# Attention and two MLP layers on one core: the softmax's division moved from the weights to the output

## The chip, the cores and the metric

The kernel runs on one core of a Trainium2 chip. The metric is the device time of one execution in microseconds (us), lower is better. The core's engines are named as the profile names them: PE (matrix multiply; PEld are its weight loads), DVE (vector), ACT (scalar), POOL (GpSimd) and SP, whose queue issues the transfers.

## The reference

```python
q_rot, k_rot = (rotate(q), rotate(k))          # rotary embedding, 4 x 8 heads, 576 positions, 64 wide
scores = scale * np.matmul(q_rot, k_rot.transpose(0, 1, 3, 2))
scores = scores - np.max(scores, axis=-1, keepdims=True)
attn = np.exp(scores)
attn = attn / (np.sum(attn, axis=-1, keepdims=True) + 1e-09)
x = np.matmul(attn, v)                         # then 2304 tokens x 512
h = x @ w_in;  x = elu(h) @ w_out              # layer 1, d_ff 2048
h = x @ w_in2; out = (h - np.tanh(h)) @ w_out2 # layer 2, d_ff 2048
```

All inputs and the output are float32.

## The kernel before

**Attention.** The 32 heads are taken as 16 pairs. A pair has nine items (`items`): four blocks of 128 query rows for each of its two heads, and one item of 128 rows that holds the last 64 rows of both. The loop over `i` goes through all 144 items, and each turn writes out a few steps of several items, so that the engines' queues are staggered. In turn i these are, in this order: the row maximum of item i on DVE (`emit_max`), the copies out of PSUM that the last turn left over (`flush`), the score matmuls of item i+1 (`emit_s`, tile s), the exponential of item i on ACT with its row sum `den` (`emit_exp`, tile a), the normalization of item i-1 (`emit_norm`), parts of the rotary work of later pairs (`prep`), the transposes of item i-D on PE into PSUM tiles pt and pr (`emit_t`, D = 4), and the products with v for a finished group of rows (`emit_pv`, tile o). The order on each engine's queue is the order of this loop; `sched` says in which turn a pair's loads and prep steps stand.

`emit_norm` runs once for two items (one at the pair's end): DVE adds 1e-9 to the two row sums (L243) and takes their reciprocals (L244), and POOL multiplies the 128x576 weights of each head in place (L247). The copies out of PSUM (L261 on DVE, L263 on ACT) are dealt out in turn, six of a pair's fifteen to DVE. The attention output o leaves PSUM as two float32r parts: ACT casts it to `xh` (L274), and a turn later DVE subtracts to get `xl` (L266). These two are the layers' input. A prep is five steps for q and five for k of a pair: two multiplications with the rotary tables (L143, mostly POOL), their sum on DVE (L145), a float32r copy on ACT (L148) and the remainder on DVE (L153), and the result goes by transfers to the places from which PE reads it.

**Layers.** Each of 192 steps takes 384 tokens and 128 of d_ff: 12 matmuls over the parts `xh`, `xl` (`emit_f1`, L441), the activation on ACT, DVE and POOL, and four steps later the second product (`emit_f2`, L498 in layer 1, L500 in layer 2). `conv_w` turns the weights into two float32r parts (L77 to L97); eight of these conversions lie in attention, over two pairs each.

Of the kernel before, what the change touches and what calls it, by code (L numbers as in the profile page):

```python
# [24 lines left out]
def attention_elu_tanhshrink(ctx: ExitStack, tc: tile.TileContext, qk, v, w1i, w1o, w2i, w2o, tab, out):  # L25
# [76 lines left out]
    with ExitStack() as actx:  # L102
# [17 lines left out]
        def load_qk(p, x):  # L120
            if p == 1 and x == 0:
                t = p3.tile([128, 2, S], F32, tag="a", name="t0")
            else:
                t = (p1, p2)[x].tile([128, 2, S], F32, tag=f"t{x}", name=f"t{x}")
            nc.sync.dma_start(out=t, in_=qk[p, :, 2 * x:2 * x + 2, :])
            t_t[p, x] = t
# [6 lines left out]
        def prep(p, x, i):  # L133
            t = t_t[p, x]
            mul = SCALE if p > 0 and x == 0 else 1.0
            if i < 2:
                if p == 0 and x == 0:
                    nc.vector.scalar_tensor_tensor(
                        out=t[:, i, :], in0=t[:, i, :], scalar=SCALE, in1=tabs[:, i, :], op0=ALU.mult, op1=ALU.mult
                    )  # L140
                else:
                    eng = nc.vector if p < 2 and i == 1 else nc.gpsimd
                    eng.tensor_tensor(out=t[:, i, :], in0=t[:, i, :], in1=tabs[:, i, :], op=ALU.mult)  # L143
            elif i == 2:
                nc.vector.tensor_tensor(out=t[:, 0, :], in0=t[:, 0, :], in1=t[:, 1, :], op=ALU.add)  # L145
            elif i == 3:
                hl_t[p, x] = p1.tile([128, 2, S], F32R, tag=f"hl{x}", name=f"hl{x}")
                nc.scalar.mul(hl_t[p, x][:, 0, :], t[:, 0, :], mul)  # L148
# [86 lines left out]

        def emit_norm(i):
# [20 lines left out]
        def flush():  # L257
# [6 lines left out]
            late.clear()  # L264
            for x0, hp, o, n in late_l:
                nc.vector.tensor_tensor(  # L266
                    out=xl[:, hp, x0:x0 + n], in0=o[:, 0:n], in1=xh[:, hp, x0:x0 + n].bitcast(F32),
                    op=ALU.subtract,
                )
            late_l.clear()  # L270
            for p, grp, o, n in late_x:
                b, hp = divmod(p, 4)
                x0 = b * S + 256 * grp
                nc.scalar.copy(out=xh[:, hp, x0:x0 + n], in_=o[:, 0:n])  # L274
                late_l.append((x0, hp, o, n))
            late_x.clear()

        def emit_t(i):
# [3 lines left out]
            if (u % 2 == 0) and h in (0, None):  # L282
                if grp < 2:
                    aT_t[p, grp] = (p2.tile([128, 2, 4, 256], F32, tag="aT", name="aT"),
                                    p2.tile([128, 256], F32, tag="aTr", name="aTr"))
                else:
                    aT_t[p, grp] = (p1.tile([128, 2, 4, 64], F32, tag="aT2", name="aT2"),
                                    p1.tile([128, 64], F32, tag="aTr2", name="aTr2"))
            aT, aTr = aT_t[p, grp]
# [5 lines left out]
            if h is None:  # L295
                for hh in range(2):
                    evac(aT[:, hh, :, 0:64], pt[:, :, 64 * hh:64 * hh + 64])
                pr = ps_t.tile([128, 4, 128], F32, tag="pt", name="pr")
                for hh in range(2):
                    sl = slice(64 * hh, 64 * hh + 64)  # L300
                    nc.tensor.matmul(out=pr[sl, 0, 0:64], lhsT=a[sl, 0, 512:576], rhs=ident[sl, sl],
                                     start=True, stop=True)
                evac(aTr[:, 0:64], pr[:, 0, 0:64])
                return
            evac(aT[:, h, :, q0:q0 + 128], pt)
            if h == 1:
                pr = ps_t.tile([128, 4, 128], F32, tag="pt", name="pr")
                nc.tensor.transpose(pr[:, 0, :], a.rearrange("p h s -> p (h s)")[:, 512:640], ident)
                evac(aTr[:, q0:q0 + 128], pr[:, 0, :])

        o_t = {}

        def emit_pv(p, grp, c):
# [6 lines left out]
            for h in range(2):  # L320
# [3 lines left out]
                else:  # L324
                    w, m = vt[sl, 512:576], aTr[sl, 0:n]
                nc.tensor.matmul(out=o[sl, 0:n], lhsT=w, rhs=m, start=(c == 0), stop=(c == 4))  # L326
# [4 lines left out]
            if grp == 2:  # L331
                v_t.pop(p)
            late_x.append((p, grp, o, n))
# [6 lines left out]
        early = {1: ((None, 0, 0, 1, 2, 3), (None, 0, 0, 0, 1, 2)), 2: ((2, 4, 5, 7, 7, 8), (4, 7, 9, 11, 12, 13))}  # L340
        for p in range(1, NPAIR):
            i0 = NI * (p - 1)
            for x in range(2):
                when = [i0 + o for o in ((-8, -6, -4, -3, -2, -1), (-7, -2, 0, 2, 3, 4))[x]]
                if p in early:
# [6 lines left out]
        with tc.manual_schedule():  # L352
            for x in range(2):
                t = t_t[0, x] = (p1, p2)[x].tile([128, 2, S], F32, tag=f"t{x}", name=f"t{x}")
                for i in range(2):
# [76 lines left out]
    def emit_f1(i):  # L432
# [72 lines left out]
    def emit_acc():  # L505
        while y_done:
            l, g, t, ys = y_done.pop()
            for e, y in enumerate(ys):
# [11 lines left out]
                if l == 0:  # L520
                    xs = slice(NB * t, NB * t + NB)
                    nc.scalar.copy(out=xh[:, e, xs], in_=a)
                    nc.gpsimd.tensor_tensor(
                        out=xl[:, e, xs], in0=a, in1=xh[:, e, xs].bitcast(F32), op=ALU.subtract
                    )
                else:
# [6 lines left out]
    with tc.manual_schedule():  # L533
# [80 lines left out]
```

## Time and profile before

| | |
|---|---|
| median of 3 runs | 1145.89 us (1145.56 to 1146.97) |
| the profiled execution, its own time | 1145.03 us |
| its span, first to last instruction | 1143.2 us |
| attention, up to the unbroken run of layer 1's matmuls | 0 to 325.06 us |
| PE busy, share of the span | 1100.3 us, 96% |
| DVE | 844.6 us, 74% |
| ACT | 612.9 us, 54% |
| POOL | 655.9 us, 57% |

The page's shares are means over two stages that are unlike each other. PE's busy time has modelled ends, so that neighbouring matmuls overlap in it; a near-full PE there isn't a proof that it never waits. For a stage the windows, the chain of waits and the timeline are read.

### The profile page before, as it was taken

The page shows a single profiled execution, that of the slowest core. Times are in us where ns is not written, and L with a number is a line of the kernel's source. Part 1 is how long each engine was busy: PE and PEld are TensorE (multiplying, and loading weights), DVE is VectorE, ACT ScalarE, POOL GpSimd, SP SyncE. Part 2 cuts the span into 40 slices and gives each one's busy share as a digit, 9 for nine tenths or more (in the row PEclk, how much of TensorE's full clock was granted, in tenths as well). Part 3 has the DMA queues.
Part 4 walks back from the last instruction along what each step waited for, and adds up shares of the span by engine and source line. Part 5 has one row for each costly group of instructions (what it writes and reads, how often), then busy time and mean ns, then how long its engine had stood idle before and what let it go on. Part 6 is the DMA issues. An engine that isn't in the chain of part 4 may idle for free.

```text
span 1143.2 us, 18404 instructions
## 1 busy us (share of the span) xinstructions
PE 1100.3 (96%) x6656; PEld 982.2 (86%) x6656; DVE 844.6 (74%) x1477; ACT 612.9 (54%) x1383; POOL 655.9 (57%) x585
## 2 busy tenths in 40 slices
PE   2899999999999999999999999999999999999998
PEld 2677776777789999999999999988999888999997
DVE  6998889888744334545544566898899999999775
ACT  3677777767634433333333343657766565655553
POOL 3877787778433333333333555866666566666553
PEclk9999999999999999999999999999999999999999
DMA  7767776766211111111111111011111111110102
GB/s 235 192 191 193 200 178 189 205 189 176 71 38 38 37 56 38 37 53 41 38 37 57 37 38 53 22 38 56 38 38 37 38 47 47 38 38 1 56 31 81
DMA packets 29627, 91.96 MB, mean 80 GB/s; under 512 B 4192, under 2 KB 4192, under 8 KB 29536
## 3 DMA queue, kind: packets, MB, share of 16 engines
q1 hardware_dynamic: 29536, 90.78, 27.6%
q8 instruction: 53, 0.87, 0.3%
q14 instruction: 38, 0.31, 0.1%
HBM read 57.74 MB, written 4.72 MB: 55 GB/s over the span
## 4 chain that ended last, share of the span: by engine, by line
PE 72%; DVE 21%; POOL 2%; ACT 2%; issue 1%; DMA 1%; SPq 1%; DVEq 0%; ACTq 0%
PE h L441 28%; PE y L498 17%; PE y L500 11%; PE o L326 6%; PE s L208 5%; PE pt L294 4%; DVE nm L217 3%; DVE f L476 3%; DVE w L475 2%; DVE f L84 2%; DVE aT L261 2%; DVE f L80 1%; DVE acc L517 1%; DVE hl L153 1%; DVE mask L474 1%
## 5 line engine op out<-in xcount | busy, mean ns | idle before, releaser
L441 PE MATMUL h<-xh,w 128*128 128x384 f32 x1536 | 424.1, 337 | 0.0
L483 POOL TENSOR_TENSOR g<-f,g 128x384 fp32r<-128x384 f32 x192 | 215.6, 1124 | 240.3 <-ACT g L482 240.2
L441 PEld LDWEIGHTS h<-xh,w 128*128 128x128 f32 x1536 | 281.7, 188 | 4.4
L441 PE MATMUL h<-xl,w 128*128 128x384 f32 x768 | 258.2, 336 | 0.0
L500 PE MATMUL y<-w,g 128*128 128x512 f32 x864 | 219.2, 399 | 7.7 <-DVE acc L517 4.6
L498 PE MATMUL y<-g,w 128*128 128x384 f32 x1152 | 215.2, 336 | 0.0
L498 PEld LDWEIGHTS y<-g,w 128*128 128x128 f32 x1152 | 201.1, 188 | 0.0
L500 PEld LDWEIGHTS y<-w,g 128*128 128x128 f32 x864 | 161.8, 189 | 40.0 <-DVE acc L517 5.7
L247 POOL TENSOR_SCALAR a<-a,r 128x576 f32<-128x576 f32 x144 | 132.2, 931 | 67.6 <-DVE r L244 49.9
L482 ACT CAST g<-f 128x384 fp32r<-128x384 f32 x192 | 99.3, 517 | 133.3 <-PE y L498 94.6
L468 DVE TENSOR_SCALAR f<-f 128x384 f32<-128x384 f32 x96 | 39.2, 408 | 147.9 <-ACT f L450 147.9
L441 PEld LDWEIGHTS h<-xl,w 128*128 128x128 f32 x768 | 144.6, 188 | 4.2
L458 POOL TENSOR_TENSOR q<-q,u 128x384 f32<-128x384 f32 x96 | 110.5, 1151 | 55.7 <-ACT q L457 55.5
L97 POOL TENSOR_TENSOR w<-f,w 128x512 fp32r<-128x512 f32 x64 | 87.9, 1374 | 90.7 <-ACT w L96 90.3
L217 DVE TENSOR_REDUCE nm<-s 128x1 f32<-128x576 f32 x144 | 108.0, 750 | 33.9 <-PE s L208 33.0
L231 ACT ACTIVATE a<-s,nm 128x576 f32<-128x576 f32 x144 | 107.5, 747 | 40.4 <-DVE nm L217 31.9
L450 ACT ACTIVATE f<-h 128x384 f32<-128x384 f32 x96 | 47.3, 492 | 147.8 <-PE h L441 141.0
L517 DVE TENSOR_TENSOR acc<-y,acc 128x384 f32<-128x384 f32 (+1 forms) x126 | 72.8, 611 | 47.1 <-PE y L498 40.8
L476 DVE COPY_PREDICATED f<-mask,w 128x384 f32<-128x384 uint8 x96 | 101.4, 1056 | 3.3
L143 POOL TENSOR_TENSOR t<-t,tabs 128x576 f32<-128x576 f32 x59 | 88.2, 1496 | 18.9 <-DMA t<-in_qk 15.8
L294 PE MATMUL pt<-ident,a 128*128 128x128 f32 x576 | 89.4, 278 | 3.9 <-ACT aT L263 2.7
L456 ACT ACTIVATE u<-h 128x384 f32<-128x384 f32 x96 | 47.3, 492 | 83.3 <-PE h L441 82.9
(56 smaller groups left out, 1498.7 us busy)
## 6 DMA issues: line engine op xcount, KB each, us to landing
k<-hl SPq DMA_DIRECT2D x64, 288.0 KB, 4.6
t<-in_qk SPq DMA_DIRECT2D x30, 576.0 KB, 4.9
raw<-in_w1i SPq DMA_DIRECT2D x16, 512.0 KB, 3.7
raw<-in_w1o SPq DMA_DIRECT2D x16, 512.0 KB, 3.6
raw<-in_w2i SPq DMA_DIRECT2D x16, 512.0 KB, 3.7
raw<-in_w2o SPq DMA_DIRECT2D x16, 512.0 KB, 3.6
v<-in_v SPq DMA_DIRECT2D x16, 288.0 KB, 5.0
qa<-hl SPq DMA_DIRECT2D x32, 144.0 KB, 2.3
```

The source lines that it names most:

```text
L143: eng.tensor_tensor(out=t[:, i, :], in0=t[:, i, :], in1=tabs[:, i, :], op=ALU.mult)
L217: nc.vector.tensor_reduce(out=nm, in_=s_t[i][:, :, 0:288], axis=AX.XY, op=ALU.max, negate=True)
L231: nc.scalar.activation(out=a.rearrange("p (x c) -> p x c", x=2), in_=s[:, :, 0:288], func=AF.Exp, bias=nm_t.pop(i), scale=1.0, accum_out=den,)
L247: nc.gpsimd.tensor_scalar(out=a, in0=a, scalar1=r[:, x:x + 1], scalar2=1.0, op0=ALU.mult, op1=ALU.mult)
L294: nc.tensor.transpose(pt[:, c, :], a[:, h or 0, c0:c0 + 128], ident)
L441: nc.tensor.matmul(out=hp, lhsT=w[:, wp, ws], rhs=x[:, c, xs], start=(m == 0), stop=(m == 3 * KC - 1))
L458: nc.gpsimd.tensor_tensor(out=q, in0=q, in1=u, op=ALU.mult)
L476: nc.vector.copy_predicated(f, mask, w)
L482: nc.scalar.copy(out=g[:, 0, :], in_=f)
L483: nc.gpsimd.tensor_tensor(out=g[:, 1, :], in0=f, in1=g[:, 0, :].bitcast(F32), op=ALU.subtract)
L498: nc.tensor.matmul(out=y_t[e][:, 0:NB], lhsT=w[:, wp, es], rhs=gt[:, gp, :], start=st, stop=sp)
L500: nc.tensor.matmul(out=y_t[e], lhsT=gt[:, gp, es], rhs=w[:, wp, :], start=st, stop=sp)
```

## The change

The weights a are no longer normalized. `emit_recip` adds 1e-9 to the row sums one column at a time and writes the reciprocals spread over 128 columns, 64 for each head of the two (128 for the last item). PE transposes this tile beside the remainder of the weights into one PSUM tile, which is copied out as a twice as wide aTr, and DVE multiplies o by it while it leaves PSUM (`flush_o`) into `xa`, which is float32. The float32r parts of `xa` are made by `split_x`: for the first 384 tokens near the end of attention, for the others in the first 20 steps of layer 1. `xa` is also the layers' accumulator. With the normalization off the way, D goes from 4 to 2. The remainder of q and k (before L153) goes from DVE to POOL for all pairs but the first, and the factor 1/8 goes from there into a second rotary table, `tabq`, made on POOL at the start. Loads of q stand two turns earlier, and weight loads at other turns.

```diff
+    xa = const.tile([128, KC * NTOK], F32, name="xa")
+    x_t = {0: const.tile([128, 2, KC, NB], F32R, name="x0")}
+    def split_x(t, c):
+        a = xa[:, NTOK * c + NB * t:NTOK * c + NB * t + NB]
+        x = x_t[t]
+        nc.scalar.copy(out=x[:, 0, c, :], in_=a)
+        nc.gpsimd.tensor_tensor(out=x[:, 1, c, :], in0=a, in1=x[:, 0, c, :].bitcast(F32), op=ALU.subtract)
...
-                nc.vector.scalar_tensor_tensor(
-                    out=hl[:, 1, :], in0=t[:, 0, :], scalar=mul, in1=hl[:, 0, :].bitcast(F32),
-                    op0=ALU.mult, op1=ALU.subtract,
+                eng = nc.vector if p == 0 else nc.gpsimd
+                eng.tensor_tensor(
+                    out=hl[:, 1, :], in0=t[:, 0, :], in1=hl[:, 0, :].bitcast(F32), op=ALU.subtract
                 )
...
-            r = sm.tile([128, 2], F32, tag="r", name="r")
-            nc.vector.tensor_scalar_add(den, den, 1e-9)
-            nc.vector.reciprocal(out=r[:, 0:nh], in_=den)
+            r = r_t[p, u] = sm.tile([128, 128], F32, tag="r", name="r")
             for x in range(nh):
-                a = a_t[p, u][:, x, :]
-                nc.gpsimd.tensor_scalar(
-                    out=a, in0=a, scalar1=r[:, x:x + 1], scalar2=1.0, op0=ALU.mult, op1=ALU.mult
-                )
+                nc.vector.tensor_scalar_add(den[:, x:x + 1], den[:, x:x + 1], 1e-9)
+            nc.vector.reciprocal(
+                out=r.rearrange("p (h d) -> p h d", h=nh), in_=den.unsqueeze(2).broadcast_to([128, nh, 128 // nh])
+            )
...
-            for x0, hp, o, n in late_l:
-                nc.vector.tensor_tensor(
-                    out=xl[:, hp, x0:x0 + n], in0=o[:, 0:n], in1=xh[:, hp, x0:x0 + n].bitcast(F32),
...
-                nc.scalar.copy(out=xh[:, hp, x0:x0 + n], in_=o[:, 0:n])
...
+        def flush_o():
+            for p, grp, o, aTr, n in late_o:
...
+                for sl, r in ((slice(0, 128), aTr[:, 1, :]),) if grp < 2 else (
+                        (slice(0, 64), aTr[0:64, 0, 64:128]), (slice(64, 128), aTr[64:128, 0, 128:192])):
+                    nc.vector.tensor_tensor(out=xa[sl, x0:x0 + n], in0=o[sl, 0:n], in1=r, op=ALU.mult)
...
-                evac(aTr[:, q0:q0 + 128], pr[:, 0, :])
+                pr = ps_t.tile([128, 512], F32, tag="pt", name="pr")
+                nc.tensor.transpose(pr[:, 0:128], a.rearrange("p h s -> p (h s)")[:, 512:640], ident)
+                nc.tensor.transpose(pr[:, 128:256], r_t.pop((p, u)), ident)
+                evac(aTr[:, :, q0:q0 + 128], pr[:, 0:256].rearrange("p (x c) -> p x c", x=2))
...
-        D = 4
+        D = 2
...
+            nc.gpsimd.tensor_scalar(out=tabq, in0=tabs, scalar1=SCALE, scalar2=1.0, op0=ALU.mult, op1=ALU.mult)
             load_v(0)
             make_identity(nc, ident)
...
+            if i < NJ * (NT - 1):
+                split_x(i // NJ + 1, i % NJ)
```

The change moves instructions on three engines. On DVE, in the middle of attention, in a stretch with steps of every kind (nm is the row maximum, xl and xa the attention output, hl the remainder of q or k), there stood before:

```order
L217 TENSOR_REDUCE nm<-s 128x1
L243 TENSOR_SCALAR den<-den 128x2
L244 RECIPROCAL r<-den 128x2
L145 TENSOR_TENSOR t_916<-t_916 128x576
L217 TENSOR_REDUCE nm<-s 128x1
L261 COPY aT<-pt 128x4x128
L266 TENSOR_TENSOR xl<-o,xh 128x256
L217 TENSOR_REDUCE nm<-s 128x1
L261 COPY aT_1220<-pt 128x256
L243 TENSOR_SCALAR den<-den 128x2
L244 RECIPROCAL r<-den 128x2
L153 SCALAR_TENSOR_TENSOR hl_1215<-t_916,hl_1215 128x576
```

and about the same place, from the copy of a 256-wide aT on, now reads:

```order
L265 COPY aT_1183<-pt 128x256
L249 TENSOR_SCALAR den<-den 128x1 x2
L250 RECIPROCAL r<-den 128x128
L150 TENSOR_TENSOR t_942<-t_942 128x576
L222 TENSOR_REDUCE nm<-s 128x1
L265 COPY aT<-pt 128x4x128
L222 TENSOR_REDUCE nm<-s 128x1
L265 COPY aTr<-pr 128x2x128
L249 TENSOR_SCALAR den<-den 128x1 x2
L250 RECIPROCAL r<-den 128x128
L276 TENSOR_TENSOR xa<-o,aTr 128x256
L276 TENSOR_TENSOR xa<-o,aTr_1184 64x64 x2
```

The remainder hl and the subtraction for xl are gone from DVE; the row sums are taken in single columns, the reciprocal is 128 wide, and the product into xa is new.

On PE, at the change from one pair to the next (pt and pr are transposes, s scores, o products with v), there stood before:

```order
L294 MATMUL pt<-ident,a 128x128 x4
L308 MATMUL pr<-ident,a 128x128
L208 MATMUL s<-k_1256,qa_97 128x288 x4
L294 MATMUL pt<-ident,a 128x128 x4
L326 MATMUL o<-aT,v 64x256 x6
```

and now:

```order
L295 MATMUL pt<-ident,a 128x128 x4
L310 MATMUL pr<-ident,a 128x128
L311 MATMUL pr<-ident,r 128x128
L213 MATMUL s<-k_1029,qa_97 128x288 x4
L295 MATMUL pt<-ident,a 128x128 x4
```

One transpose of r follows each transpose of the remainder, ahead of the next scores; there are five in a pair.

On POOL, at the start of the program (ident is the identity for the transposes, t the rotary products of q or k), there stood before:

```order
masks.py:199 AFFINE_SELECT ident<-ident 128x128
L143 TENSOR_TENSOR t_107<-t_107,tabs 128x576
L143 TENSOR_TENSOR t_110<-t_110,tabs 128x576
L143 TENSOR_TENSOR t_112<-t_112,tabs 128x576
L247 TENSOR_SCALAR a<-a,r 128x576 x4
```

and now:

```order
L364 TENSOR_SCALAR tabq<-tabs 128x1152
masks.py:197 MEMSET ident 128x128
masks.py:199 AFFINE_SELECT ident<-ident 128x128
L148 TENSOR_TENSOR t_108<-t_108,tabs 128x576
L148 TENSOR_TENSOR t_111<-t_111,tabq 128x576
L148 TENSOR_TENSOR t_113<-t_113,tabs 128x576
L159 TENSOR_TENSOR hl_178<-t_113,hl_178 128x576
```

The second table stands ahead of the identity and of the first pair's k, and the remainders hl follow where the normalization of a stood.

## Rows read from the trace of the kernel before

**Rows 1.** Windows of attention and layers: length, busy us of each engine (instructions), clock, DMA.

```profile
60.00:290.00 230.00, 222.82 (x1811) 164.65 (x1810) 206.05 (x423) 165.34 (x412) 182.29 (x167) 1.00 0.69 188
317.20:1143.20 826.00, 814.56 (x4388) 770.48 (x4386) 576.05 (x933) 400.16 (x858) 426.58 (x368) 1.00 0.13 42
```

**Rows 2.** Windows of three pairs of heads, from one PE position to the same.

```profile
130.09:148.49 18.40, 18.01 (x146) 13.30 (x147) 16.10 (x35) 13.40 (x34) 13.64 (x13) 1.00 0.75 208
...
sum 55.40, PE 53.91 PEld 39.86 DVE 49.42 ACT 40.04 POOL 43.48; mean PE 17.97 PEld 13.29 DVE 16.47 ACT 13.35 POOL 14.49
```

**Rows 3.** Chain of waits, same three pairs: shares by line, then pieces (start, us, what).

```profile
by line: PE o L326 20.4%; PE s L208 14.8%; DVE nm L217 13.8%; PE pt L294 11.1%; DVE aT L261 6.6%; DVE den L243 4.3%; DVE f L80 4.2%; issue 4.1%; ACT aT L263 3.4%; ACT hl L148 3.1%; DVE hl L153 2.7%; DVE t L145 2.7%; ACT a L231 2.4%; DVE f L
...
136.40 0.44 PE pt L294 x4
136.84 0.11 PE pr L308
...
157.51 1.20 DVE den L243
```

**Rows 4.** Groups of instructions, whole run, shapes apart, DVE: count, busy us, mean ns.

```profile
L153 DVE SCALAR_TENSOR_TENSOR hl<-t,hl 128x576 fp32r<-128x576 f32 x32 | 27.5, 861 | 3.1 <-ACT hl L148 2.0
L243 DVE TENSOR_SCALAR den<-den 128x2 f32<-128x2 f32 x64 | 26.3, 410 | 0.0
L266 DVE TENSOR_TENSOR xl<-o,xh 128x256 fp32r<-128x256 f32 x32 | 13.3, 414 | 2.7 <-ACT xh L274 2.7
L244 DVE RECIPROCAL r<-den 128x2 f32<-128x2 f32 x64 | 10.6, 166 | 2.4
L261 DVE COPY aTr<-pr 128x128 f32<-128x128 f32 x32 | 8.9, 278 | 0.0
L266 DVE TENSOR_TENSOR xl<-o,xh 128x64 fp32r<-128x64 f32 x16 | 3.4, 215 | 0.2 <-ACT xh L274 0.2
L244 DVE RECIPROCAL r<-den 128x1 f32<-128x1 f32 x16 | 2.6, 164 | 0.6
L243 DVE TENSOR_SCALAR den<-den 128x1 f32<-128x1 f32 x16 | 2.3, 145 | 0.5 <-ACT a L231 0.5
```

**Rows 5.** Timeline of POOL and DVE around one row sum: start, us, engine, line.

```profile
157.26 1.42 POOL L143 TENSOR_TENSOR t<-t,tabs 128x576 f32<-128x576 f32 x1
...
157.43 1.27 DVE L243 TENSOR_SCALAR den<-den 128x2 f32<-128x2 f32 x1
158.74 0.17 DVE L244 RECIPROCAL r<-den 128x2 f32<-128x2 f32 x1
```

**Rows 6.** Groups of instructions, whole run: POOL's normalization and copies of ACT.

```profile
L247 POOL TENSOR_SCALAR a<-a,r 128x576 f32<-128x576 f32 x144 | 132.2, 931 | 67.6 <-DVE r L244 49.9 <-PE s L208 7.7 <-ACT a L231 2.5
L523 POOL TENSOR_TENSOR xl<-acc,xh 128x384 fp32r<-128x384 f32 x24 | 26.7, 1142 | 6.0 <-ACT xh L522 6.0
L274 ACT CAST xh<-o 128x256 fp32r<-128x256 f32 (+1 forms) x48 | 15.3, 319 | 30.1 <-PE o L326 30.1
```

**Rows 7.** Timeline of PE: the same place in the last two pairs of heads.

```profile
286.74 1.51 PE L326 MATMUL o<-aT,v 128*64 128x256 f32 x12
...
304.90 1.51 PE L326 MATMUL o<-aT,v 128*64 128x256 f32 x12
```

**Rows 8.** Timeline of the start: DVE, POOL and the first scores on PE.

```profile
6.86 0.76 DVE L138 SCALAR_TENSOR_TENSOR t<-t,tabs 128x576 f32<-128x576 f32 x1 [1.57 <-DMA tabs<-in_tab]
7.66 0.76 DVE L145 TENSOR_TENSOR t<-t 128x576 f32<-128x576 f32 x1
7.82 1.86 POOL L143 TENSOR_TENSOR t<-t,tabs 128x576 f32<-128x576 f32 x1 [6.51 <-DMA t<-in_qk]
...
10.40 1.76 DVE L145 TENSOR_TENSOR t<-t 128x576 f32<-128x576 f32 x1
```

**Rows 9.** Timeline of attention's end on PE and its weight loads.

```profile
314.69 0.63 PE L294 MATMUL pt<-ident,a 128*128 128x128 f32 x4 [0.66 <-ACT aT L263]
...
316.69 0.42 PEld L294 LDWEIGHTS pt<-ident,a 128*128 128x128 f32 x4 [0.39 <-POOL a L247]
```

More of the change, by code (lines that the diff above doesn't have):

```diff
@@ L113, in attention_elu_tanhshrink @@
         tabs = acst.tile([128, 2, S], F32, name="tabs")
+        tabq = acst.tile([128, 2, S], F32, name="tabq")
         zero = acst.tile([128, 64], F32, name="zero")
@@ L120, in load_qk @@
         def load_qk(p, x):
[L121 to L124, printed above, removed]
+            t = p2.tile([128, 2, S], F32, tag=f"t{x}", name=f"t{x}")
             nc.sync.dma_start(out=t, in_=qk[p, :, 2 * x:2 * x + 2, :])
@@ L134, in prep @@
             t = t_t[p, x]
-            mul = SCALE if p > 0 and x == 0 else 1.0
             if i < 2:
@@ L142, in prep @@
                     eng = nc.vector if p < 2 and i == 1 else nc.gpsimd
-                    eng.tensor_tensor(out=t[:, i, :], in0=t[:, i, :], in1=tabs[:, i, :], op=ALU.mult)
+                    tb = (tabq, tabs)[x]
+                    eng.tensor_tensor(out=t[:, i, :], in0=t[:, i, :], in1=tb[:, i, :], op=ALU.mult)
             elif i == 2:
@@ L147, in prep @@
                 hl_t[p, x] = p1.tile([128, 2, S], F32R, tag=f"hl{x}", name=f"hl{x}")
-                nc.scalar.mul(hl_t[p, x][:, 0, :], t[:, 0, :], mul)
+                nc.scalar.copy(out=hl_t[p, x][:, 0, :], in_=t[:, 0, :])
             else:
@@ L234, in emit_exp, with emit_recip @@
             )
-        def emit_norm(i):
+        def emit_recip(i):
             p, u, h = items[i]
@@ L264, in flush @@
             late.clear()
-            for x0, hp, o, n in late_l:
-                nc.vector.tensor_tensor(
-                    out=xl[:, hp, x0:x0 + n], in0=o[:, 0:n], in1=xh[:, hp, x0:x0 + n].bitcast(F32),
[L268 to L271, printed above, removed]
-                b, hp = divmod(p, 4)
-                x0 = b * S + 256 * grp
-                nc.scalar.copy(out=xh[:, hp, x0:x0 + n], in_=o[:, 0:n])
-                late_l.append((x0, hp, o, n))
-            late_x.clear()
+        def flush_o():
+            for p, grp, o, aTr, n in late_o:
+                b, hp = divmod(p, 4)
+                x0 = NTOK * hp + b * S + 256 * grp
+                for sl, r in ((slice(0, 128), aTr[:, 1, :]),) if grp < 2 else (
+                        (slice(0, 64), aTr[0:64, 0, 64:128]), (slice(64, 128), aTr[64:128, 0, 128:192])):
+                    nc.vector.tensor_tensor(out=xa[sl, x0:x0 + n], in0=o[sl, 0:n], in1=r, op=ALU.mult)
+            late_o.clear()
         def emit_t(i):
@@ L284, in emit_t @@
                     aT_t[p, grp] = (p2.tile([128, 2, 4, 256], F32, tag="aT", name="aT"),
-                                    p2.tile([128, 256], F32, tag="aTr", name="aTr"))
+                                    p2.tile([128, 2, 256], F32, tag="aTr", name="aTr"))
                 else:
                     aT_t[p, grp] = (p1.tile([128, 2, 4, 64], F32, tag="aT2", name="aT2"),
-                                    p1.tile([128, 64], F32, tag="aTr2", name="aTr2"))
+                                    p1.tile([128, 1, 192], F32, tag="aTr2", name="aTr2"))
             aT, aTr = aT_t[p, grp]
@@ L297, in emit_t @@
                     evac(aT[:, hh, :, 0:64], pt[:, :, 64 * hh:64 * hh + 64])
-                pr = ps_t.tile([128, 4, 128], F32, tag="pt", name="pr")
+                pr = ps_t.tile([128, 512], F32, tag="pt", name="pr")
                 for hh in range(2):
                     sl = slice(64 * hh, 64 * hh + 64)
-                    nc.tensor.matmul(out=pr[sl, 0, 0:64], lhsT=a[sl, 0, 512:576], rhs=ident[sl, sl],
+                    nc.tensor.matmul(out=pr[sl, 0:64], lhsT=a[sl, 0, 512:576], rhs=ident[sl, sl],
                                      start=True, stop=True)
-                evac(aTr[:, 0:64], pr[:, 0, 0:64])
+                nc.tensor.transpose(pr[:, 64:192], r_t.pop((p, u)), ident)
+                evac(aTr[:, 0, :], pr[:, 0:192])
                 return
@@ L306, in emit_t @@
             if h == 1:
-                pr = ps_t.tile([128, 4, 128], F32, tag="pt", name="pr")
-                nc.tensor.transpose(pr[:, 0, :], a.rearrange("p h s -> p (h s)")[:, 512:640], ident)
-                evac(aTr[:, q0:q0 + 128], pr[:, 0, :])
+                pr = ps_t.tile([128, 512], F32, tag="pt", name="pr")
+                nc.tensor.transpose(pr[:, 0:128], a.rearrange("p h s -> p (h s)")[:, 512:640], ident)
+                nc.tensor.transpose(pr[:, 128:256], r_t.pop((p, u)), ident)
+                evac(aTr[:, :, q0:q0 + 128], pr[:, 0:256].rearrange("p (x c) -> p x c", x=2))
         o_t = {}
@@ L324, in emit_pv @@
                 else:
-                    w, m = vt[sl, 512:576], aTr[sl, 0:n]
+                    w, m = vt[sl, 512:576], aTr[sl, 0, 0:n]
                 nc.tensor.matmul(out=o[sl, 0:n], lhsT=w, rhs=m, start=(c == 0), stop=(c == 4))
@@ L332, in emit_pv @@
                 v_t.pop(p)
-            late_x.append((p, grp, o, n))
-        D = 4
+            late_o.append((p, grp, o, aTr, n))
+        D = 2
         NDIRECT = 2
@@ L343, in attention_elu_tanhshrink @@
             for x in range(2):
-                when = [i0 + o for o in ((-8, -6, -4, -3, -2, -1), (-7, -2, 0, 2, 3, 4))[x]]
+                when = [i0 + o for o in ((-10, -6, -4, -3, -2, -1), (-7, -2, 0, 2, 3, 4))[x]]
                 if p in early:
@@ L353, in attention_elu_tanhshrink @@
             for x in range(2):
-                t = t_t[0, x] = (p1, p2)[x].tile([128, 2, S], F32, tag=f"t{x}", name=f"t{x}")
+                t = t_t[0, x] = p2.tile([128, 2, S], F32, tag=f"t{x}", name=f"t{x}")
                 for i in range(2):
@@ L372, in attention_elu_tanhshrink @@
             pend = []
+            nw = list(range(len(first_w)))[::-1]
             emit_s(0)
@@ L382, in attention_elu_tanhshrink @@
                         f(*arg)
-                if r == 0 and p % 2 == 0 and p // 2 < len(first_w):
-                    load_w(first_w[p // 2])
+                if i == 1 or i % (2 * NI) == 12:
+                    load_w(first_w[nw.pop()]) if nw else None
                 if i < n:
@@ L392, in attention_elu_tanhshrink @@
                 if 0 <= i - 1 < n:
-                    emit_norm(i - 1)
+                    emit_recip(i - 1)
+                flush_o()
                 if p < NPAIR:
@@ L410, in attention_elu_tanhshrink @@
                     pend.remove(x)
+                if n - 8 <= i < n and (i - n) % 2 == 0:
+                    split_x(0, (i - n + 8) // 2)
             while pend:
@@ L413, in attention_elu_tanhshrink @@
             flush()
-            flush()
+            flush_o()
     w_p2 = ctx.enter_context(tc.tile_pool(name="w_b", bufs=1))
@@ L425, in attention_elu_tanhshrink @@
     ps_y = ctx.enter_context(tc.tile_pool(name="ps_y", bufs=4, space=PSUM))
-    acc = fcst.tile([128, KC * NTOK], F32, name="acc")
+    for t in range(1, NT):
+        x_t[t] = fcst.tile([128, 2, KC, NB], F32R, name=f"x{t}")
+    acc = xa
     b1 = fcst.tile([128, 1], F32, name="b1")
@@ L438, in emit_f1 @@
             ws = slice(128 * c, 128 * c + 128)
-            xs = slice(NB * t, NB * t + NB)
-            for wp, x in ((0, xh), (0, xl), (1, xh)):
-                nc.tensor.matmul(out=hp, lhsT=w[:, wp, ws], rhs=x[:, c, xs], start=(m == 0), stop=(m == 3 * KC - 1))
+            for wp, xp in ((0, 0), (0, 1), (1, 0)):
+                nc.tensor.matmul(
+                    out=hp, lhsT=w[:, wp, ws], rhs=x_t[t][:, xp, c, :], start=(m == 0), stop=(m == 3 * KC - 1)
+                )
                 m += 1
@@ L520, in emit_acc @@
                 if l == 0:
[L521 to L525, printed above, removed]
+                    split_x(t, e)
                 else:
```

7 lines of the change are left out of this document (3 added, 4 removed).

## The prediction

> **What bounds the kernel now.** I read the stages first. In attention PE is busy 222.8 of 230 us and DVE 206 (90%), POOL 182; in the layers PE 814.6 of 826 and DVE only 576 [rows 1]. [...] The layers keep PE full, and the change leaves their matmuls as they are. What it can win or lose is in the first 325 us.
>
> A pair of heads takes 18.47 us (55.40 for three), with 16.47 of DVE and 14.49 of POOL [rows 2]. PE's 17.97 there has modelled ends and says little, so I go to the chain of waits of the same stretch [rows 3]. It changes sides: PE lines (o, s, pt) hold 46% of it, DVE lines over a third (34% in the names shown; I use 36%), ACT 9%. Attention is bound by PE and DVE in turn: whoever has the longer list in a turn of the loop keeps the other waiting. So an edit on either engine counts with about the share of the chain that the engine holds, and what stands in the chain by name counts more.
>
> Two DVE names there are touched by the change: the row sums `den` (4.3%) and the remainder hl (2.7%). A row sum of two columns takes 410 ns in the mean, one of a single column 145 [rows 4]. The timeline tells why: at 157.43 it takes 1.27 us while POOL's rotary product runs from 157.26 to 158.68, and it ends 0.02 us later [rows 5]. The two-column form waits for POOL, and the next maximum waits behind it.
>
> **DVE, per pair.** Off: four two-column sums, 64 x 410 ns / 16 = 1.64; two remainders, 27.5 / 16 = 1.72; the subtraction for xl, (13.3 + 3.4) / 16 = 1.04; five reciprocals, (10.6 + 2.6) / 16 = 0.83; two narrow aTr copies at 278 ns, 0.56. The one-column sum at the pair's end stays. Sum 5.79. On: eight more one-column sums at 145 ns, 1.16. Products into xa: two of 256 columns and, for the last group, two of 64, as the xl subtraction costs (414 and 215 ns), 1.26. Two aTr copies of 256 columns: 128 more columns at 1.04 ns, the slope between those two forms (199 ns for 192 columns), 0.82. Five reciprocals of 128 columns, for which the trace has only 1 and 2 columns, 164 and 166 ns [rows 4]. Between 1.04 ns a column and 3 ns (the 2 ns between these rows and one for rounding) that is 0.30 to 0.54 us; I take 0.35, near the step that was read and the slope of other operations, so 1.75. Sum 4.99. Net: -0.8 us of DVE a pair; with 0.54 for a reciprocal it is +0.1.
>
> [...]
>
> **PE, per pair.** Five more transposes of 128 x 128, each 0.11 us as pr takes in the chain (0.44 for four pt) [rows 3]: +0.55 us, +8.8 for the 16 pairs. Nothing on PE is removed. They stand behind pr, which already waits for a copy out, and ahead of the next scores, which wait for an exponential; so part falls into waits. I let PE's share of the chain count, 46%: +0.25 a pair; the bounds are nothing and all of it.
>
> **How the two add up.** What stood in the chain is freed: of the row sums the waiting, (410 - 145) ns x 4 = 1.06 a pair if each stood on it, 0.8 by its 4.3% of 18.47, and the remainder's 0.5. What is added on DVE without a name in the chain (one-column sums, wider reciprocals and copies, products against xl, less what they replace: 0.5 + 0.9 + 0.25 + 0.2 = 1.85) counts with 36%, +0.7. That makes -0.6 on DVE, +0.25 on PE: -0.35 a pair. There is a check on how much relief is to be had: between the last two equal places of PE, when part of the rotary work has run out, a pair takes 18.16 [rows 7], 0.31 under the mean. So relief of DVE alone meets a next limit, the loop from scores to maximum to exponential, after some 0.3 us, and against the transposes' 0.25 that leaves -0.06. I take the middle, **-0.2 a pair, -3.2 us for 16**; the bounds are -0.6 (DVE's relief whole, transposes hidden: -9.6) and +0.55 (no relief, transposes in full: +8.8).
>
> **The start.** POOL makes `tabq` when both tables have landed, about 6.8 us. Its 1152 columns cost up to twice the 0.93 us of a 576-column pass [rows 6], and the identity and the first pair's k follow, where k's product now starts at 7.82. DVE's operations at 6.86 and 7.66 read two tiles and can hold up POOL or be held up, as the 1.76 us of the 0.76-us sum at 10.40 shows [rows 8]. k's product starts 1.0 to 2.5 us later: +1.5. Two remainders of pair 1 leave DVE in this DVE-bound stretch: -0.7.
>
> **The end.** With D = 2 fewer items are left after the last scores, and no transposes wait for POOL: two waits of 0.66 and 0.39 us stand there [rows 9]. -0.6, bounds 0 and -1.2.
>
> **What I cost at nothing.** POOL loses 132.2 us of normalization [rows 6] and gets 30 remainders at about its 1.4-us rotary product [rows 5], 42 us: it is no limit. ACT loses 15.3 us of casts [rows 6] and gets 128 more columns in three copies a pair, some 6 us in all. In layer 1 twenty steps get a cast and a 1.14-us subtraction on POOL [rows 6], in steps of 826 / 192 = 4.3 us with POOL busy 52% and ACT 48% [rows 1]: covered, and needed only a step later. Were the cover gone, PE would wait 20 x 1.14 = 23 us. SP's transfers are the same in number but for the order; the moved loads stand earlier.
>
> Sum: -3.2 + 1.5 - 0.7 - 0.6 = -3.0 against the profiled execution's own 1145.03 (span 1143.2), so **1142.0**. The median of the runs shown stands 0.86 above that execution, well inside the range.
>
> **The rivals.** (1) *The transposes are paid in full.* PE is the fuller engine; if the loop of scores and exponentials already was the limit in most turns, DVE's relief brings little, and with 8.8 for the transposes, -2 of relief, start and end +0.2, the time is **1152** (1148 to 1154). For it: 18.16 in the lightly loaded pair. Against: DVE's share of the chain. Slower; it decides where relief is under about 0.3 us a pair.
> (2) *They cancel.* Relief and transposes meet at about nothing, and start and end decide: **1145** (1143.5 to 1148). A form of it: POOL, no longer paced by reciprocals, runs ahead with two-tile products and holds up DVE's sum t and the weights' conversion instead; `f L80` has 4.2% of the chain [rows 3].
> (3) *The reciprocal is dear.* DVE has 18.47 - 16.47 + 0.8 = 2.8 us a pair free with 0.35 us; beyond 0.35 + 2.8 / 5 = 0.9 us each it is the bound, and every further 0.1 us costs 8 us. [...]
> (4) *More is freed.* The bursts of DVE (sum, copy, conversion, row sum in succession) were what held PE, and without them attention runs as PE alone allows: -9.6 and the end, about **1135**.
> That the change does not do what it says has no room: the order of instructions shows it.
>
> **Chances.** Forecast (1138 to 1143.5) 0.38; (1) 0.20; (2) 0.26; (3) 0.06; (4) 0.10. The range leaves out (3), half of (4) and the far end of (1): 1135 to 1152. About 0.2%, 2.3 us, is what a measurement here can tell from no change, so faster begins below 1143.6 and slower above 1148.2. Faster: 0.38 + 0.10 = 0.48. Slower: 0.20 + 0.06 = 0.26. The same: 0.26. The forecast's own range is 1138 to 1143.5.
>
> **What would show it.** Right: the reciprocal r at 0.30 to 0.40 us; `den` at 0.14 with no waits; a pair at 18.2 to 18.3 us; DVE at 15.5 to 16 a pair; transposes of r at 0.11; layer 1 without PE gaps; the first scores 1 to 2 us later. Wrong: a reciprocal over 0.6; DVE sums t or conversions with new waits for POOL; a pair at 18.6 or more with DVE idle before the maxima (then rival 1); a stop of PE at the fifth step of layer 1.

## The result and the profile after

| | before | after |
|---|---|---|
| median of 4 runs each | 1145.72 us (1144.76 to 1146.97) | 1160.72 us (1159.47 to 1161.70) |
| ratio | 1 | 1.0130, 95% interval 1.0112 to 1.0147 |
| span of the profiled execution | 1143.2 us | 1157.7 us |
| start of layer 1's unbroken matmuls | 325.06 us | 339.65 us |

The change makes the kernel 15.0 us slower; 1142.0 had been forecast, with a range of 1135 to 1152. The profile of the changed kernel follows in the order of the prediction. First come the windows of the same stretch of attention and of three pairs (length, then busy us of PE, PEld, DVE, ACT, POOL, clock, DMA):

```profile
60.00:290.00 230.00, 219.09 (x1777) 161.53 (x1775) 212.21 (x437) 148.41 (x353) 104.67 (x76) 1.00 0.66 178
130.72:189.56 58.84, 56.51 (x457) 41.94 (x458) 53.45 (x110) 38.50 (x91) 26.65 (x20) 1.00 0.67 179
```

Against [rows 1] DVE is busier, 212 for 206 us, while POOL has lost 78 us and ACT 17. A pair takes 58.84 / 3 = 19.61 us for 18.47 [rows 2], and its DVE time is 17.82 for 16.47, where the prediction said 15.5 to 16. The clock is 1.00 in both.

The chain of waits at attention's end, changed kernel (start, us, what):

```profile
336.32 3.33 PE o L329 x40
339.65 9.58 PE h L450 x54
```

and in the kernel before:

```profile
325.06 9.58 PE h L441 x54
```

From there to the end of the span it took 1143.2 - 325.06 = 818.1 us before, and now 1157.7 - 339.65 = 818.1. The layers are unchanged, the splitting in layer 1 included: all of the loss (14.6 us up to that place, 14.5 in the whole span) lies in attention. The groups of instructions that answer to [rows 4], changed kernel, shapes apart (count, busy us, mean ns, idle before):

```profile
L250 DVE RECIPROCAL r<-den 128x128 f32<-128x128 f32 x80 | 76.2, 953 | 2.7
L249 DVE TENSOR_SCALAR den<-den 128x1 f32<-128x1 f32 x144 | 15.3, 144 | 0.2
L265 DVE COPY aTr<-pr 128x256 f32<-128x256 f32 x32 | 13.3, 415 | 0.5 <-PE pr L311 0.5
L276 DVE TENSOR_TENSOR xa<-o,aTr 128x256 f32<-128x256 f32 x32 | 11.6, 363 | 3.2 <-PE o L329 3.2
L276 DVE TENSOR_TENSOR xa<-o,aTr 64x64 f32<-64x64 f32 x32 | 7.1, 222 | 3.6 <-PE o L329 3.4
L159 POOL TENSOR_TENSOR hl<-t,hl 128x576 fp32r<-128x576 f32 x30 | 42.3, 1412 | 102.2 <-ACT hl L153 102.2
```

Five of six stand about where they were put: row sums at 144 ns, copies at 415, products at 363 and 222, POOL's remainders at 1.41 us. The reciprocal takes 953 ns, where 350 was taken and 540 the bound. The chain of waits shows what that does in a pair (pieces of `issue`, 0.04 us at most, are left out):

```profile
134.80 0.76 DVE nm L222
135.56 0.60 DVE aT L265
136.16 0.13 DVE den L249 x2
136.31 0.95 DVE r L250
137.26 0.61 DVE nm L222
137.88 0.07 DVE den L249
137.97 0.95 DVE r L250
138.92 0.28 DVE xa L276
139.19 0.66 DVE nm L222
139.86 0.61 DVE aT L265
140.51 0.33 PE pr L302 x4
```

From 134.80 to 140.51 the chain is DVE's alone, with a reciprocal on either side of one maximum. PE's next transposes, and the products behind them, wait for the copies that follow, and the exponentials wait for the maxima. Shares by line over the three pairs of the window above, against [rows 3]:

```profile
by line: PE o L329 22.7%; DVE nm L222 17.6%; PE s L213 15.8%; DVE r L250 9.8%; DVE aT L265 8.2%; DVE f L86 4.3%; PE pt L295 3.7%; issue 2.7%; PE pr L302 1.7%; PE pr L310 1.7%; DVE f L87 1.5%; DVE xa L276 1.4%; PE pr L304 1.3%; ACT a L236 1.
```

`hl` (2.7% before) has left the chain as forecast. `den` (4.3% before) is down to 1.2%: its pieces add up to 0.73 of the 58.84 us. `r` has come in with 9.8%, and the maxima rose from 13.8 to 17.6%. The same in waits of ACT over 60 to 290 us (in total, times, longest), first after, then before:

```profile
ACT a L236 <- DVE nm L222: 38.5, 41, 1.3
ACT a L231 <- DVE nm L217: 21.2, 24, 1.6
```

The start that answers to [rows 8], timeline of the changed kernel:

```profile
6.82 1.70 POOL L364 TENSOR_SCALAR tabq<-tabs 128x1152 f32<-128x1152 f32 x1 [6.38 <-DMA tabs<-in_tab]
9.24 1.89 POOL L148 TENSOR_TENSOR t<-t,tabs 128x576 f32<-128x576 f32 x1
11.17 1.94 DVE L150 TENSOR_TENSOR t<-t 128x576 f32<-128x576 f32 x1 [1.29 <-POOL t L148]
```

The second table takes 1.70 us, k's product starts 1.42 us later than at 7.82, and DVE's sum behind it 0.77 later than at 10.40.

### The profile page after: what moved, and what is told of

It reads as the page before. It is cut to its first block, busy times and chain, and to the rows that moved or that the text cites. A ratio compares the mean times of both kernels' runs of the same rounds, so it can differ in the third digit from the quotient of the medians.

```text
span 1157.7 us, 18311 instructions
## 1 busy us (share of the span) xinstructions
PE 1110.2 (96%) x6736; PEld 990.0 (86%) x6736; DVE 881.3 (76%) x1527; ACT 612.9 (53%) x1359; POOL 587.8 (51%) x496
## 4 chain that ended last, share of the span: by engine, by line
PE 68%; DVE 25%; POOL 3%; ACT 2%; issue 1%; DMA 1%; SPq 0%; POOLq 0%; ACTq 0%
PE h L450 27%; PE y L509 16%; PE y L511 11%; PE o L329 6%; DVE nm L222 5%; PE s L213 4%; DVE f L487 3%; DVE r L250 3%; DVE w L486 2%; DVE aT L265 2%; DVE f L91 2%; DVE xa L528 1%; PE pt L295 1%; DVE f L86 1%; DVE f L95 1%
## 5 line engine op out<-in xcount | busy, mean ns | idle before, releaser
L450 PE MATMUL h<-x,w 128*128 128x384 f32 x2304 | 435.3, 337 | 0.0
L450 PEld LDWEIGHTS h<-x,w 128*128 128x128 f32 x2304 | 408.4, 189 | 8.5
L469 POOL TENSOR_TENSOR q<-q,u 128x384 f32<-128x384 f32 x96 | 110.6, 1152 | 55.8 <-ACT q L468 55.5
L528 DVE TENSOR_TENSOR xa<-y,xa 128x384 f32<-128x384 f32 (+1 forms) x126 | 72.9, 611 | 46.8 <-PE y L509 40.8
L159 POOL TENSOR_TENSOR hl<-t,hl 128x576 fp32r<-128x576 f32 x30 | 42.3, 1412 | 102.2 <-ACT hl L153 102.2
L486 DVE SCALAR_TENSOR_TENSOR w<-w,q 128x384 f32<-128x384 f32 x96 | 80.2, 835 | 7.2 <-POOL q L469 7.2
L329 PE MATMUL o<-aT,v 128*64 128x256 f32 (+1 forms) x768 | 80.1, 337 | 0.0
L250 DVE RECIPROCAL r<-den 128x128 f32<-128x128 f32 x80 | 76.2, 953 | 2.7
```

What stands on the lines that cost most here:

```text
L250: nc.vector.reciprocal(out=r.rearrange("p (h d) -> p h d", h=nh), in_=den.unsqueeze(2).broadcast_to([128, nh, 128 // nh]))
L450: nc.tensor.matmul(out=hp, lhsT=w[:, wp, ws], rhs=x_t[t][:, xp, c, :], start=(m == 0), stop=(m == 3 * KC - 1))
L469: nc.gpsimd.tensor_tensor(out=q, in0=q, in1=u, op=ALU.mult)
L486: nc.vector.scalar_tensor_tensor(out=w, in0=w, scalar=G1, in1=q, op0=ALU.add, op1=ALU.mult)
```

## The experiments

"Changed kernel" is the one after; the kernel before had medians of 1145.3 to 1145.9 us beside these runs. A ratio is against it, with its 95% interval.

### What one reciprocal costs: `widths`

Reciprocals of many widths, three of each, stand behind the last step of the changed kernel, where nothing waits for them.

```diff
+        for w in (1, 2, 4, 8, 12, 16, 32, 64, 96, 128, 256, 384):
+            for rep in range(3):
+                q = tmp3.tile([128, NB], F32, tag="f", name="rcp")
+                nc.vector.reciprocal(out=q[:, 0:w], in_=xa[:, 0:w])
...
```

> The changed kernel with reciprocals of 1 to 384 columns, three of each, added on DVE behind the last step, where nothing else runs. By rows of the profile after, 953 ns for 128 columns against 164 and 166 ns for 1 and 2 before. If the cost is linear with a floor, about 6.2 ns a column above some 4 to 10 columns, 0.56 us at 64 and 2.5 us at 384; if it comes in batches of 8 columns, 8 columns cost as 1 and then steps appear; if the spread source (step 0) is what costs, 128 plain columns take 0.3 us.

Groups by shape at the end of that run, DVE (`rcb` reads two columns spread by step 0 to 128, `rcc` are copies):

```profile
L569 DVE RECIPROCAL rcp<-xa 128x384 f32<-128x384 f32 x3 | 7.3, 2495 | 0.0
L569 DVE RECIPROCAL rcp<-xa 128x256 f32<-128x256 f32 x3 | 4.9, 1695 | 0.0
L573 DVE RECIPROCAL rcb<-xa 128x128 f32<-128x128 f32 x3 | 2.6, 907 | 0.0
L569 DVE RECIPROCAL rcp<-xa 128x128 f32<-128x128 f32 x3 | 2.5, 895 | 0.0
L569 DVE RECIPROCAL rcp<-xa 128x64 f32<-128x64 f32 x3 | 1.3, 495 | 0.0
L569 DVE RECIPROCAL rcp<-xa 128x32 f32<-128x32 f32 x3 | 0.7, 295 | 0.0
L569 DVE RECIPROCAL rcp<-xa 128x16 f32<-128x16 f32 x3 | 0.4, 196 | 0.0
L569 DVE RECIPROCAL rcp<-xa 128x8 f32<-128x8 f32 x3 | 0.3, 165 | 0.0
L569 DVE RECIPROCAL rcp<-xa 128x2 f32<-128x2 f32 x3 | 0.3, 151 | 0.0
L569 DVE RECIPROCAL rcp<-xa 128x1 f32<-128x1 f32 x3 | 0.3, 147 | 0.0
L577 DVE COPY rcc<-xa 128x128 f32<-128x128 f32 x3 | 0.5, 218 | 0.0
```

From 16 columns on the rows lie on one line: (2495 - 295) / (384 - 32) = 6.25 ns a column, plus 95 ns. A copy of 128 columns takes 218 ns, so the width alone isn't what costs. The spread source isn't either: 907 against 895. By that line one column would take 101 ns and two 107; this run has 147 and 151, and 165 at eight, and the kernel before has 164 and 166 [rows 4]. Both lie on a floor, and a slope taken between them says nothing of the slope above.

### The same change with narrow reciprocals: `narrow_pool`, `narrow_act`

DVE takes the reciprocal of one or two columns; POOL, or ACT, copies it to the 128 columns. The rest is the changed kernel.

```diff
-            nc.vector.reciprocal(
-                out=r.rearrange("p (h d) -> p h d", h=nh), in_=den.unsqueeze(2).broadcast_to([128, nh, 128 // nh])
+            r2 = sm.tile([128, 2], F32, tag="r2", name="r2")
+            nc.vector.reciprocal(out=r2[:, 0:nh], in_=den)
+            nc.scalar.copy(
+                out=r.rearrange("p (h d) -> p h d", h=nh), in_=r2[:, 0:nh].unsqueeze(2).broadcast_to([128, nh, 128 // nh])
             )
```

> The changed kernel with the reciprocals taken over 1 or 2 columns again; POOL spreads them to 128 columns by a copy. Dear reciprocal (each of 0.95 us on DVE holds the pair at 19.6 us): DVE loses 5 x 0.79 = 3.9 us a pair, the pair falls to 18.1 to 18.4 us and the time to 1138 to 1145. Transposes paid in full (PE is the limit and DVE only looks full): the time falls by less than 5 us, to 1156 or more. A third reading, a loop from scores to maximum to exponential that is longer with D = 2: also little, above 1152.

> The same with the spreading copy on ACT. Dear reciprocal: 1138 to 1145 as with POOL, a few us more if the copy delays the exponentials (5 x 0.25 us a pair on ACT, 20 us in all if none of it is hidden). Transposes in full, or a longer loop: above 1152. If POOL and ACT differ by over 5 us, the place of the copy matters, not DVE alone.

Measured: 1147.92 us with POOL's copy (ratio 1.0022, 1.0013 to 1.0032) and 1147.13 with ACT's (1.0013, 1.0003 to 1.0022). Both lie 2 to 3 us above the 1138 to 1145 that a dear reciprocal was expected to give, and well below the 1152 or more of the other readings. Of the 15.0 us lost, 13.6 come back with ACT's copy, when the width of 80 reciprocals is changed and 80 copies of 0.30 us are added on ACT. The window of `narrow_act`, and under it its chain of waits over three pairs:

```profile
60.00:290.00 230.00, 226.87 (x1852) 168.88 (x1852) 182.80 (x453) 163.73 (x430) 107.69 (x78) 1.00 0.68 182
```

```profile
by line: PE o L331 32.5%; PE s L213 29.8%; PE pt L297 17.7%; ACT a L236 4.0%; ACT aT L269 3.1%; PE pr L312 2.9%; DVE nm L222 2.7%; DVE aT L267 2.2%; PE pr L313 1.7%; PE pr L304 1.5%; PE pr L306 1.4%; issue 0.7%
```

DVE is down to 183 of 230 us and, in the names shown, to 5% of the chain; PE's lines now hold 88%. What is left over the kernel before is 1.4 us.

### Only the wide reciprocal, in the kernel before: `before_wide`

POOL reads two of the 128 columns, and the wider tile r has two buffers where the narrow one had six (left out here).

```diff
...
-            nc.vector.reciprocal(out=r[:, 0:nh], in_=den)
+            nc.vector.reciprocal(
+                out=r.rearrange("p (h d) -> p h d", h=nh), in_=den.unsqueeze(2).broadcast_to([128, nh, 128 // nh])
+            )
...
```

> The kernel before with one thing changed: its reciprocals are written over 128 columns, as in the changed kernel (POOL reads two of the columns; two buffers for them). DVE gets 5 x 0.79 = 3.9 us a pair where 2.0 are free. Dear reciprocal: a pair goes to 20 us or more and the time to 1168 to 1185. If DVE had room and other parts of the change made the loss: under 1155.

Measured: 1169.44 us (1.0201, 1.0186 to 1.0216), 23.8 us more. Its window, its reciprocals in the groups of instructions, and its chain of waits over 60 to 290 us:

```profile
60.00:290.00 230.00, 206.67 (x1647) 150.33 (x1644) 222.54 (x385) 149.22 (x374) 161.69 (x153) 1.00 0.64 176
```

```profile
L245 DVE RECIPROCAL r<-den 128x128 f32<-128x128 f32 x80 | 76.2, 953 | 6.6 <-DVE den L244 0.5
```

```profile
by line: DVE nm L218 19.3%; issue 10.8%; DVE aT L264 8.7%; DMA k<-hl 8.5%; DVE hl L154 7.8%; DVE r L245 5.4%; PE o L329 4.6%; DVE t L146 3.9%; DMA v<-in_v 3.8%; SPq L176 3.5%; DVE den L244 3.5%; PE s L209 3.0%; ACT aT L266 2.8%; ACT a L232 
```

DVE is busy 97% of the stretch. Waiting for one of the two buffers isn't what costs: DVE's idle time ahead of all 80 reciprocals is 6.6 us. The wide reciprocal costs more alone (23.8) than within the change (13.6). The rest of the change takes work off DVE, which fits; and here the remainder `hl`, still on DVE, and the transfer of k behind it hold 7.8 and 8.5% of the chain. How the difference divides between the two stays open.

### The transposes of r: `no_r_transpose`, `narrow_act_no_t`

The five transposes of a pair go, so that the output isn't divided by the row sums, and the copies out keep their width (they read the weights' transpose over again). The first is the changed kernel without them, the second `narrow_act` without them.

```diff
...
-                nc.tensor.transpose(pr[:, 128:256], r_t.pop((p, u)), ident)
-                evac(aTr[:, :, q0:q0 + 128], pr[:, 0:256].rearrange("p (x c) -> p x c", x=2))
+                r_t.pop((p, u))
+                evac(aTr[:, :, q0:q0 + 128], pr[:, 0:128].unsqueeze(1).broadcast_to([128, 2, 128]))
```

> The changed kernel without the 80 transposes of r; the reciprocals are still computed, the copies out are as wide, and the output is multiplied by columns of the transposed weights instead of the reciprocals. Dear reciprocal: PE has room, so at most half of the 80 x 0.11 = 8.7 us comes back, 1156 to 1160.5. Transposes in full: 8 us or more come back, 1152 or less.

> Narrow reciprocals spread by ACT, and no transposes of r (the output is multiplied by columns of the transposed weights instead). With the narrow reciprocals the chain of waits is 88% PE, so the transposes should now be paid in full: 16 x (0.55 to 0.65) = 9 to 10 us less than the 1147.1 of the narrow kernel, 1136.5 to 1139, and a pair at 18.1 to 18.2 us. If the loop from scores to exponential is the limit instead: under 5 us less, 1142 or more.

Measured: 1155.32 us (1.0083, 1.0068 to 1.0098), 5.4 under the changed kernel; and 1140.65 (0.9952, 0.9935 to 0.9969), 6.5 under `narrow_act`. The transposes take 0.11 us each, as forecast; in the changed kernel's chain of waits, at attention's end:

```profile
333.93 0.11 PE pr L310
334.05 0.11 PE pr L311
```

By the medians, of 80 x 0.11 = 8.8 us 61% are paid where DVE is the fuller engine and 74% where PE is; the prediction had let 46% count. Each difference is uncertain by over 2 us (the two ratios' intervals together), so the two shares can't be told apart, and the first doesn't exclude 46%. Both lie between the cases that the expectations had named: at most half or 8 us and more, and 9 to 10 us or under 5.

### The row sums in single columns: `before_single_sums`, `narrow_act_pair_sums`

The one part of the change that relieves DVE's wait for POOL, alone in the kernel before; and undone in `narrow_act`.

```diff
-            nc.vector.tensor_scalar_add(den, den, 1e-9)
+            for x in range(nh):
+                nc.vector.tensor_scalar_add(den[:, x:x + 1], den[:, x:x + 1], 1e-9)
```

> The kernel before with one thing changed: 1e-9 is added to the row sums one column at a time, as in the changed kernel, so that they no longer wait for POOL. The prediction's claim on DVE's relief: 1.06 us a pair leave DVE and, capped by the next limit, 0.2 to 0.35 us a pair leave the time: 1140 to 1143, below both kernels. If the waiting was hidden behind PE: 1144.5 to 1147.

> Narrow reciprocals spread by ACT, and the row sums of two columns in one instruction as before. POOL is busy 47% of attention there against 79% before, so a two-column sum should wait less often than 410 ns in the mean, 250 to 350. With room on DVE: 1146 to 1149. If waits for POOL stand on the path even so: 1150 or more.

Measured: the kernel before with this one edit takes **1141.76 us** (0.9969, 0.9958 to 0.9981), 3.6 under it in the same runs, and is faster than both kernels of this case. Its row sums in the groups of instructions, and its chain of waits over three pairs:

```profile
L244 DVE TENSOR_SCALAR den<-den 128x1 f32<-128x1 f32 x144 | 15.3, 143 | 0.5 <-ACT a L231 0.5
```

```profile
by line: PE o L327 17.9%; PE s L208 16.2%; DMA t<-in_qk 10.1%; PE pt L295 9.9%; DMA k<-hl 8.5%; DVE nm L217 6.4%; DVE hl L153 4.1%; ACT a L231 3.8%; issue 3.7%; SPq L178 2.9%; DVE f L79 2.4%; DVE aT L262 2.2%; ACT hl L148 2.1%; SPq L175 1.9
```

Two single columns take at most 0.29 us where a two-column sum took 0.41, and the mean of 143 ns over all 144 leaves no room for waits like the 1.27 us of [rows 5]. In the kernel before, 25 of the 64 two-column sums take 0.51 to 1.27 us; each of them begins while a rotary product of POOL (L143) runs and ends 0.02 to 0.04 us after it. The other 39 take 0.15 to 0.17 us. In the changed kernel two single-column sums together span 0.20 to 0.22 us, also where an operation of POOL runs all the while, as L159 does for 1.41 us from 174.20 around the two at 175.29. Why two columns wait for POOL and one doesn't, no run shows. In `narrow_act` the two-column form costs less, 1148.11 us (1.0025, 1.0016 to 1.0035), 1.0 more and within the intervals, though a sum takes still longer there, where 250 to 350 ns had been expected (groups of instructions):

```profile
L248 DVE TENSOR_SCALAR den<-den 128x2 f32<-128x2 f32 x64 | 29.5, 460 | 0.2
```

DVE isn't what holds that kernel.

### Depth, copies, remainders: `after_d4`, `narrow_act_copies`, `narrow_act_copies_d4`, `narrow_act_hl_dve`

```diff
-        D = 2
+        D = 4
...
-                if ev[0] % 5 in (1, 3):
+                if ev[0] % 15 in (1, 3, 4, 6, 8, 11, 13):
...
-                eng = nc.vector if p == 0 else nc.gpsimd
+                eng = nc.vector
```

The first hunk alone makes `after_d4` of the changed kernel; in `narrow_act` the second makes `narrow_act_copies`, the first two `narrow_act_copies_d4`, the third `narrow_act_hl_dve`.

> The changed kernel with D = 4 as before. If the shorter distance between exponential and transposes makes part of the loss (a transpose that waits, a loop that closes sooner), the time falls by 3 us or more, under 1157.5. If the wide reciprocals hold DVE, D moves nothing: 1159 to 1162.5.

> Narrow reciprocals spread by ACT, and one more of a pair's fifteen copies out of PSUM on DVE (seven instead of six), the one after which ACT's exponential is late once a pair. If that wait costs PE, 16 x 0.2 to 0.4 = 3 to 6 us less than 1147.1: 1141 to 1144, below the kernel before. If PE's own work is the limit: 1146 to 1148.

> Narrow reciprocals spread by ACT, seven copies on DVE, and D = 4. If D = 2 costs because steps bunch on DVE (as after_d4 had it, 4.5 us), it costs less where DVE has room: 1142 to 1146. If PE's own work sets the time: 1145 to 1147.5, as with D = 2.

> Narrow reciprocals spread by ACT, and the remainders of q and k back on DVE (1.4 us a pair). With PE as the limit (88% of the chain) DVE has room: 1146 to 1149.5, no change from 1147.1. If DVE's relief is what pays for the transposes: 1150 or more.

`after_d4`: 1156.24 us (1.0087, 1.0072 to 1.0102), 4.5 less than with D = 2. That is the first of the two cases named: the shorter distance between exponential and transposes makes part of the loss, beside wide reciprocals. `narrow_act_copies`: 1146.09 (1.0002, 0.9993 to 1.0011), so one copy more on DVE changes next to nothing; the copies on ACT aren't what holds `narrow_act`, which fits the 88% that PE's own work has of its chain. With D = 4 besides: 1155.42 (1.0084, 1.0070 to 1.0098), 9.3 worse and above both ranges named. So D has one sign with wide reciprocals and the other with narrow ones (and seven copies on DVE). `narrow_act_hl_dve`: 1166.96 (1.0187, 1.0173 to 1.0201), 20 us worse than `narrow_act`, far into the second case, though DVE is busy only 186.5 of 230 us there. POOL's waits over 60 to 290 us (in total, times, longest) in that kernel:

```profile
POOL w L104 <- ACT w L103: 91.7, 6, 15.6
POOL t L148 <- DMA t<-in_qk: 65.9, 9, 11.4
```

and in `narrow_act`:

```profile
POOL w L104 <- ACT w L103: 29.7, 6, 5.0
POOL t L148 <- DMA t<-in_qk: 5.3, 1, 5.3
```

With the remainders on DVE, POOL stands up to 15.6 us before the weights' conversion with the next rotary products queued behind it, and the loads of q and k come late. The chain of waits of `narrow_act_hl_dve` over 60 to 290 us shows where that reaches PE:

```profile
by line: PE o L331 26.3%; PE s L213 16.6%; DMA k<-hl 9.4%; PE pt L297 8.5%; DVE nm L222 8.5%; DVE hl L159 8.2%; DVE aT L267 3.7%; SPq L180 3.2%; ACT a L236 2.6%; DVE xa L278 2.2%; PE pr L312 2.2%; issue 2.2%; DVE f L95 1.6%; PE pr L304 1.5%
```

The remainder on DVE, the issue of k's transfer behind it and the transfer (`hl`, `SPq`, `k<-hl`) hold 21% of it, and none of them stands in the chain of `narrow_act` shown above: the scores wait for a k that comes late. What starts the lateness, the remainder's place in DVE's queue or POOL's, wasn't tried, nor why D changes sign; both stay open.

## Why the prediction was wrong

**The step that failed** is in DVE's list per pair: "Five reciprocals of 128 columns, for which the trace has only 1 and 2 columns, 164 and 166 ns", taken at 0.35 us between bounds of 0.30 and 0.54. The runs show 0.953, outside the bounds and above the 0.6 that the prediction had named as a sign of being wrong. The bounds themselves were badly made: the 2 ns between two forms under the floor counted as a slope, and that a reciprocal's slope was like a copy's was a guess. With 0.953 the five take 4.77 us for 1.75, and DVE's net a pair is +2.2 by that list instead of -0.8. Measured it is +1.35 (17.82 - 16.47), so the rest of the list came out some 0.9 cheaper; the products into xa, 363 ns for 414, are a small part of that. By the prediction's own share, 36% of (953 - 350) ns x 80 = 48 us, 17.4 would be added to 1142.0: 1159.4, against 1160.72. That agreement is partly luck: the same rule for `narrow_act`, which has 0.83 us of reciprocals a pair instead of 1.75, gives 1142.0 - 0.36 x 0.92 x 16 = 1136.7, and 1147.13 was measured, with ACT's copies in it.

**Rival (3)** names the mechanism, with the wrong onset: it let a dear reciprocal cost nothing up to 0.9 us and 8 us for each 0.1 beyond, some 4 us at 0.953. In fact the cost is paid before DVE is full: a pair takes 19.61 us with DVE busy 17.82, since PE waits through bursts like that at 134.80. It got 0.06, because two rows from under the floor seemed to speak against a dear reciprocal; the run of widths shows 6.25 ns a column, and 895 ns at 128.

**The transposes:** 0.11 us each held; the share of 46% looks low, 61 and 74% by the medians. So 1142 would hardly have come with a cheap reciprocal either: `narrow_act` at 1147.13 and `narrow_pool` at 1147.92 lie where rival (2) put the time, relief and transposes cancelling, and PE's lines hold 88% of `narrow_act`'s chain. What their added copies hide of it, no run shows.

**The relief:** right in place, and of its sizes the cap held. Single-column sums alone bring 3.6 us, 0.22 a pair, under the 0.3 that the lightly loaded pair had set as a cap and far under the 0.8 to 1.06 of the chain and the rows; what stands in the chain instead, over those three pairs, is transfers of q and k (10.1 and 8.5%). The change doesn't keep this gain: `narrow_act` comes to a like time, 1140.65, only without the transposes.

**Start and end:** k's product 1.42 us later (1.0 to 2.5 forecast), the first scores at 13.16 for 12.21. That is gone by the second pair of heads, whose first exponential starts at 38.99 us for 39.30 before. At the end, D = 2 leaves 339.65 - 330.36 = 9.3 us after the last scores instead of 325.06 - 313.44 = 11.6; part of that is work that now stands ahead of them, so how much was won there stays open. D = 2 was counted only here, at -0.6; what it does within the pairs was left out, and beside wide reciprocals that costs 4.5 us (`after_d4`).

**Costed at nothing:** the split in layer 1: right, the layers took 818.1 us in both. POOL's remainders and ACT's added columns: in the names shown of the chain after, no line of POOL stands and of ACT only the exponentials, with under 2%.

## What to carry to other kernels

Price an operation per column from rows that are well above its fixed cost; two rows at one and two columns give the floor and no slope, and then the bound must reach to the dearest operation of that engine, not to the commonest. A wide reciprocal is four times a copy here (895 ns against 218 at 128 columns), so take it of the few columns that are needed and spread the result with a copy on an engine with room. Before moving a division from the weights to the output to relieve an engine, try the one edit that removes the wait seen in the chain: here single-column row sums alone beat the whole change.

## What was not expected of the hardware

DVE's float32 reciprocal takes 6.25 ns a column and about 95 ns besides (895 ns at 128 columns, 2495 at 384), and at one and two columns 147 and 151 ns in the same run, 164 and 166 in the kernel before; a copy of 128 columns takes 218. With DVE busy only some 80% of attention, the place of a step in the queues still moves this kernel by 9 to 20 us: with narrow reciprocals D = 4 for 2 gave +9.3 us and the remainders on DVE 20, where with wide ones D = 4 gave -4.5.
